# Polysketch attention with a gated feed-forward network: den in the idle accumulator bank, gating ahead of the division, one scratch write and GpSimd-issued reads, outer products of batch 0 in three pieces

## The chip, the cores and the metric

The kernel runs on one core of one Trainium2 chip. The metric is the device time of one execution in microseconds, the median of several runs. A profiled execution has its own time, and within it the span that the trace covers. Engines are named as the profile names them: PE multiplies matrices (PEld loads its weights), DVE is the vector engine, ACT the scalar engine, POOL is GpSimd, SP only issues transfers. SBUF is the memory on the core, PSUM holds what PE writes.

## The reference, cut to what matters

```python
q, k, v: (4, 4, 1088, 32)            # batch, heads, sequence, head_dim
S1, S2: (8, 32)
def phi(x):
    a = einsum('rd,bhsd->bhsr', S1, x)
    b = einsum('rd,bhsd->bhsr', S2, x)
    return einsum('bhsi,bhsj->bhsij', a, b).reshape(..., 64)
q_p, k_p = phi(q), phi(k)
kv  = einsum('bhsf,bhsd->bhfd', k_p, v)
z   = sum(k_p, axis=2)
num = einsum('bhsf,bhfd->bhsd', q_p, kv)
den = einsum('bhsf,bhf->bhs', q_p, z)[..., None] + 1e-06
x   = (num / den).transpose(0, 2, 1, 3).reshape(4352, 128)
out = (1 / (1 + exp(-(x @ w_gate))) * (x @ w_val)) @ w_out      # d_ff 1536
```

## The kernel before, in words

All arithmetic is in float32. The 4352 tokens of the feed-forward part are cut into eight chunks of 512 and one of 256. A **wave** (`w1`, L297) multiplies one chunk by one 128-wide tile of `w_gate` and of `w_val` (L309, two matmuls, four records in the trace). ACT takes the sigmoid of one half (L317), DVE multiplies it with the other (`glu`, L329, the gating, written `g`), and `w2` (L260) adds the product with the tile of `w_out` into an accumulator bank (L266). The accumulators have two PSUM banks, `acc0` and `acc1`, taken in turn by the chunks; when a chunk is done DVE turns it (L276) and SP stores it (L287). There are 102 waves. PE's queue runs `w2` two waves behind `w1`.

Between the waves stands the attention of the next batch, as groups handed to `slot` (L343): a group's instructions are issued first, then so many waves. The order of PE, DVE, ACT and POOL is the order in which the program is written; SP's queue has its own. For a batch `b`, `turn_k` and `turn_q` transpose the loaded k and q, `kps` (L386) projects k with S1 and S2, `outer` (L411) makes the 64 products of a token (`kp`), `kv` sums `kp` times `v`, `kvd` and `ndt` turn the result around into `nd` (numerator weights) and `zb` (denominator weights).

For q the products are made another way in most places: `qcomp` (L475) projects q, ACT copies the result to `cq`, `spread` (L504) writes `cq` to scratch memory in DRAM (`dq`) and reads it back twice, with rows repeated, as `qp` and `bq`; `qmult` (L539) multiplies the two on DVE. The query tokens of a batch are in two halves, `n` = 0 (8 blocks of 32 a parity) and `n` = 1 (9 blocks). `spread` does both halves of batches 1 to 3 in one go, and half 1 of batch 0 alone (`q01`). `bq` lies in the buffer that held the batch's k and q, and the next batch's k and q are loaded there after `qmult`. In batch 0, half 0, the projections are multiplied directly (`ab`).

`dn` (L636) then multiplies `qp` by `zb` (L644, the denominator) and by `nd` (L654, the numerator) into one two-bank PSUM tile of the pool `ps2`; for half 1 the denominator has to be cut into two pieces to fit beside the numerator. `divide` (L662) is six DVE steps: transposition of the denominator (`dT`, L665), + 1e-6 (L670), reciprocal (L671), transposition back (`rb`, L675), product with the numerator (`xT`, L684), and `xT` is what the waves multiply.

The weights come as 64-bit floating point words in pairs of 32-bit words and are narrowed on chip, tile by tile (`narrow`, L82, called as `narrow_w(j, step)`): POOL makes `cap` (L96), ACT `tail` (L100), DVE `head` in two instructions (L104, L108), ACT `square` (L116, into a PSUM tile that takes the bank `acc1`) and POOL adds `head` and `tail` (L117), DVE writes the float32 tile into `w_sb` (L120). Tile 0 is narrowed in two parts (`narrow_0`). Wave j of chunk 0 needs tile j, and the narrowing of the later tiles stands inside `w1` of chunk 0.

The program's start is batch 0: `outer` in four instructions (five and four of the nine key blocks), `kv0` (L544) after each, `kvd`, `ndt`, `dn(0, 0)`, `divide`, then the first wave. `warm` (L233) puts dummy matmuls on PE.

## Time and profile before

| what | value |
|---|---|
| median of 3 runs | 322.04 us (321.23 to 322.5) |
| profiled execution, its own time | 323.64 us |
| span of its trace | 321.8 us |
| PE busy | 303.6 us, 94% |
| DVE busy | 155.5 us, 48% |
| ACT busy | 80.4 us, 25% |
| POOL busy | 21.3 us, 7% |
| PE, waiting for DVE's gating (L266 behind L329) | 8.7 us in 8 waits |
| DVE, waiting for the reads of `bq` (L541) | 6.9 us in 2 waits |
| granted clock of PE, in tenths | 9 in every slice but one of 40, which has 7 |

The times of a row are the start in us from the start of the span and the length. PE's end is modelled: a matmul that follows another at once starts before the row of the one ahead has ended, so the length of a wave among others is best read from start to start. What an engine is said to wait for is the last to come; an idle stretch of an engine on which nothing waits costs nothing.

### The profile page before, as it was taken

To read this page: it belongs to the slowest core of one execution; us is meant where nothing else is said; L and a number is where in the kernel's file an instruction comes from. 1 tells how busy PE (TensorE), PEld (TensorE's weight loads), DVE (VectorE), ACT (ScalarE), POOL (GpSimd) and SP (SyncE) were. 2 spreads that over 40 slices of the span, in tenths; PEclk is the share of its full clock that TensorE was granted. 3 is DMA by queue.
4 is the path that set the end of the run, shared out by engine and by line. 5 is a ranking of instruction groups with operands and counts; after the bars stand their busy time and mean duration, and the time that the engine had idled before them with its cause. 6 is when DMAs were issued, how large, how long until landed. Compare 5 with 4: busy or idle time off the path is not lost.

```text
span 321.8 us, 3740 instructions
## 1 busy us (share of the span) xinstructions
PE 303.6 (94%) x1430; PEld 138.7 (43%) x1430; DVE 155.5 (48%) x268; ACT 80.4 (25%) x151; POOL 21.3 (7%) x36
## 2 busy tenths in 40 slices
PE   8868998999599999999999999999999999999994
PEld 2533443444234444443344444433444444444683
DVE  4778788763534645346446453464223222222331
ACT  2334552223011322221213222212122222222220
POOL 1235551000000000000000000000000000000000
PEclk9999999999979999999999999999999999999999
DMA  7990413177800257143002571010002000200021
GB/s 187 362 325 20 123 35 140 24 161 126 222 25 2 34 121 144 53 102 140 2 0 33 121 139 54 5 31 0 0 0 35 0 0 0 33 0 0 3 32 16
DMA packets 28656, 22.91 MB, mean 71 GB/s; under 512 B 19808, under 2 KB 23776, under 8 KB 28640
## 3 DMA queue, kind: packets, MB, share of 16 engines
q1 hardware_dynamic: 27712, 22.14, 27.7%
q10 hardware_dynamic: 928, 0.54, 0.8%
q8 instruction: 11, 0.18, 0.2%
q14 instruction: 5, 0.04, 0.0%
HBM read 19.46 MB, written 3.21 MB: 70 GB/s over the span
## 4 chain that ended last, share of the span: by engine, by line
PE 78%; DVE 10%; DMA 6%; issue 2%; SPq 1%; ACT 1%; POOL 1%; ACTq 0%; DVEq 0%
PE wave L309 46%; PE moeout L266 25%; DMA bq<-dq 5%; DVE rb L675 2%; DVE xT L684 2%; DVE g L329 2%; PE dn L654 1%; PE dn L644 1%; DVE dT L665 1%; DMA kq<-in_k_dram 1%; PE kvz L551 1%; PE kps L396 1%; SPq L526 1%; PE kvz L565 1%; DVE head L108 1%
## 5 line engine op out<-in xcount | busy, mean ns | idle before, releaser
L309 PE MATMUL wave<-xT,w_sb 128*128 128x512 f32 (+1 forms) x436 | 193.2, 569 | 2.5 <-DVE w_sb L120 1.5
L329 DVE TENSOR_TENSOR g<-wave,sg 128x512 f32<-128x512 f32 x102 | 70.3, 690 | 124.6 <-ACT sg L317 124.0
L309 PEld LDWEIGHTS wave<-xT,w_sb 128*128 128x128 f32 x436 | 82.9, 191 | 97.0 <-issue 89.2
L266 PE MATMUL moeout<-g,w_sb 128*128 128x512 f32 (+1 forms) x216 | 106.2, 579 | 8.7 <-DVE g L329 8.7
L317 ACT ACTIVATE sg<-wave 128x512 f32<-128x512 f32 x102 | 60.9, 597 | 213.2 <-PE wave L309 213.2
L266 PEld LDWEIGHTS moeout<-g,w_sb 128*128 128x128 f32 x216 | 39.0, 190 | 54.7 <-issue 35.3
L117 POOL TENSOR_TENSOR head<-head,tail 128x384 int32<-128x384 int32 (+3 forms) x14 | 13.4, 959 | 22.4 <-DVE head L108 12.0
L541 DVE TENSOR_TENSOR qp<-qp,bq 128x1152 f32<-128x1152 f32 (+1 forms) x7 | 9.1, 1294 | 6.9 <-DMA bq<-dq 6.9
L665 DVE STREAM_TRANSPOSE dT<-dn 128x256 f32<-128x256 f32 (+2 forms) x12 | 4.0, 357 | 14.0 <-PE dn L654 14.0
L415 DVE TENSOR_TENSOR kp<-kab 128x1152 f32<-128x1152 f32 (+2 forms) x10 | 10.7, 1096 | 0.0
L120 DVE SCALAR_TENSOR_TENSOR w_sb<-square,head 128x384 f32<-128x384 f32 x11 | 6.1, 555 | 4.4 <-POOL head L117 4.4
L108 DVE SCALAR_TENSOR_TENSOR head<-cap,head 128x384 int32<-128x384 int32 (+3 forms) x14 | 7.9, 565 | 0.5
L239 PE MATMUL warm<-ones 128*128 128x512 f32 (+1 forms) x10 | 7.2, 858 | 1.0 <-DVE hm L245 1.0
L276 DVE STREAM_TRANSPOSE o_sb<-moeout 128x512 f32<-128x512 f32 (+1 forms) x9 | 6.1, 680 | 2.6 <-PE moeout L266 2.5
L96 POOL TENSOR_SCALAR cap<-w_in 128x384 f32<-128x384 f32 (+2 forms) x13 | 7.0, 549 | 4.1 <-DMA w_in<-in_moe_w_val_dram 4.1
L100 ACT ACTIVATE tail<-w_in 128x384 int32<-128x384 uint32 (+2 forms) x13 | 6.5, 518 | 0.0
L654 PE MATMUL dn<-qp,nd 64*32 64x256 f32 (+1 forms) x128 | 6.1, 401 | 0.4 <-issue 0.4
L675 DVE STREAM_TRANSPOSE rb<-rc 128x576 f32<-128x576 f32 (+2 forms) x9 | 6.1, 680 | 0.3
L684 DVE TENSOR_TENSOR xT<-dn,rb 128x576 f32<-128x576 f32 (+2 forms) x9 | 6.0, 661 | 0.3
L373 DVE STREAM_TRANSPOSE kT<-kq 128x1088 f32<-128x1088 f32 (+2 forms) x5 | 5.4, 1070 | 1.3 <-DMA kq<-in_k_dram 1.3
L384 DVE STREAM_TRANSPOSE qT<-kq 128x512 f32<-128x512 f32 (+1 forms) x8 | 5.7, 714 | 0.0
L644 PE MATMUL dn<-qp,zb 128*32 128x256 f32 (+2 forms) x96 | 5.6, 338 | 0.1
(59 smaller groups left out, 81.7 us busy)
## 6 DMA issues: line engine op xcount, KB each, us to landing
v<-in_v_dram SPq DMA_DIRECT2D x16, 144.0 KB, 5.6
bq<-dq SPq DMA_DIRECT2D x8, 288.0 KB
qp<-dq SPq DMA_DIRECT2D x3, 576.0 KB, 10.6
kq<-in_k_dram SPq DMA_DIRECT2D x3, 544.0 KB
kq<-in_q_dram SPq DMA_DIRECT2D x3, 544.0 KB, 4.9
w_in<-in_moe_w_gate_dram SPq DMA_DIRECT2D x6, 256.0 KB
w_in<-in_moe_w_val_dram SPq DMA_DIRECT2D x6, 256.0 KB, 6.6
w_in<-in_moe_w_out_dram SPq DMA_DIRECT2D x6, 256.0 KB, 5.3
```

The costliest lines, as they stand in the source:

```text
L108: nc.vector.scalar_tensor_tensor(out=head, in0=cap, scalar=-0x40000000, in1=head, op0=ALU.bitwise_and, op1=ALU.bitwise_or)
L117: nc.gpsimd.tensor_tensor(out=head, in0=head, in1=tail, op=ALU.add)
L266: nc.tensor.matmul(out=moe["acc"][:, :tw], lhsT=w_sb[:, 2, j, :], rhs=g[:, jj, :tw], start=(j == 0), stop=(j == NJ - 1),)
L309: nc.tensor.matmul(out=wv[:, which, jj * tw + o : jj * tw + o + tp], lhsT=w_sb[:, which, j0 + jj, :], rhs=xT[:, t0 + o : t0 + o + tp], sta ...
L317: nc.scalar.activation(out=sg, in_=wv[:, 0], func=ACTF.Sigmoid)
L329: nc.vector.tensor_tensor(out=g, in0=wv[:, 1], in1=sg, op=MUL)
L415: nc.vector.tensor_tensor(out=KP[b][:, pi, j0:j1].rearrange("p j m (i l) -> p (j m) i l", i=R), in0=bass.AP(tensor=a0.tensor, offset=a0.of ...
L541: nc.vector.tensor_tensor(out=q0, in0=q0, in1=half(BQ[b], n), op=MUL)
L644: nc.tensor.matmul(out=t[32 * h : 32 * h + 32, i, w : w + 32 * (u1 - u0)], lhsT=zb[b % 2][:, h, :], rhs=half(QP[b], n)[:, 2 * (h % 2) + h ...
L654: nc.tensor.matmul(out=t[32 * h : 32 * h + 32, c, :w], lhsT=ND[b][rows, 32 * h : 32 * h + 32], rhs=half(QP[b], n)[rows, 2 * (h % 2) + h // ...
L675: nc.vector.transpose(out=rb[:, u0:u1].rearrange("p t c s -> p (t c s)"), in_=bass.AP(tensor=r0.tensor, offset=r0.offset, ap=[list(r0.ap[0 ...
L684: nc.vector.tensor_tensor(out=xT[:, o : o + 64 * (u1 - u0)].rearrange("p (t c s) -> p c t s", c=2, s=32), in0=t[:, :, 32 * u0 : 32 * u1].r ...
```

## The change

It has five parts.

1. The denominator goes into a PSUM tile of its own (`dps`), in the accumulator bank that the running chunk does not use: `acc0` or `acc1`, by the new entry `moe["sum"]`, the chunk whose `w2` began last. For half 1 it is four matmuls of 288 columns in place of eight of 224 and 64, and one transposition on DVE in place of two. The last weight tile's `square` goes to SBUF, so that `acc1` is free of it. The numerator keeps the tile of `ps2`.
2. `part` puts the gating of the wave before ahead of `dn` and `divide`, at seven of the eight divisions (all but the first of batch 0).
3. `spread` writes all of `cq` to scratch with one transfer and reads it back with eight transfers of 64 partitions (288 KB each) for both halves, four for one half. For batches 1 to 3 SP issues the write and POOL the reads; for `q01` ACT writes, SP reads. Both halves are 288 columns wide in scratch and in the buffers (`W1`), so half 0 carries 32 columns a row that nothing uses.
4. Batch 0's outer products come in six instructions (key blocks 0 to 3, 4 to 6, 7 and 8; two of the four heads in each), with `kv0` over all four heads after each pair.
5. Two steps of the narrowing of weight tile 1 stand before the first division, where they stood behind it.

```diff
+    W1 = 32 * q_chk[1][1]
...
-                narrowing[j] = narrow(w_sb[:, :, j, :], w_in[n][:, :, jj], nc.gpsimd, True)
+                narrowing[j] = narrow(w_sb[:, :, j, :], w_in[n][:, :, jj], nc.gpsimd, j < NJ - 1)
...
         if j0 == 0:
+            moe["sum"] = ci
             moe["acc"] = pso.tile([P, TCH], F32, tag=f"acc{ci % 2}", name="moeout")
...
-        w0, w1 = 32 * q_chk[0][1], 32 * q_chk[1][1]
-        if 0 in ns:
-            nc.scalar.copy(out=cq[:, :, :w0], in_=t[:, :, :w0])
-            nc.scalar.copy(out=cq[64:, :, w0:w1], in_=t[64:, :, w0:w1])
-        else:
-            nc.scalar.copy(out=cq[64:, :, :w1], in_=t[64:, :, :w1])
+        p0 = 64 * ns[0]
+        nc.scalar.copy(out=cq[p0:], in_=t[p0:, :, :W1])
...
+    def spread(b, ns, cq, put, get):
+        p0 = 64 * ns[0]
+        d = dram.tile([P, 2, W1], F32, tag="dq", name="dq")
+        put.dma_start(out=d[p0:], in_=cq[p0:])
         for n in ns:
             for c in range(2):
+                for i, t in enumerate((QP[b], BQ[b])):
+                    d0 = d[64 * n + 32 * c + 16 * i, 0]
+                    rows = [[4 * W1, R], [0, R]] if i == 0 else [[0, R], [4 * W1, R]]
+                    get.dma_start(
+                        out=t[64 * c : 64 * c + 64, n * H * W1 : (n + 1) * H * W1],
+                        in_=bass.AP(
+                            tensor=d0.tensor, offset=d0.offset, ap=rows + [[1, H * W1]]
+                        ),
                     )
...
-        t = ps2.tile([P, 2, 512], F32, tag="two", name="dn")
-        u = min(tn, (512 - w) // 32)
-        pieces = [(0, 0, u), (1, u, tn)] if u < tn else [(0, 0, tn)]
-        for i, u0, u1 in pieces:
-            for h in range(H):
-                nc.tensor.matmul(
-                    out=t[32 * h : 32 * h + 32, i, w : w + 32 * (u1 - u0)],
...
+        dps = pso.tile([P, TCH], F32, tag=f"acc{(moe['sum'] + 1) % 2}", name="dps")
+        for h in range(H):
+            nc.tensor.matmul(
+                out=dps[32 * h : 32 * h + 32, :w],
+                lhsT=zb[b % 2][:, h, :],
+                rhs=half(QP[b], n)[:, 2 * (h % 2) + h // 2, :],
+                start=True,
+                stop=True,
+            )
+        t = ps2.tile([P, 2, 512], F32, tag="two", name="nps")
...
-            for i, u0, u1 in pieces:
-                nc.vector.transpose(
-                    out=dT[:, u0:u1].rearrange("p t c -> p (t c)"),
-                    in_=t[:, i, w : w + 32 * (u1 - u0)],
-                )
+            nc.vector.transpose(out=dT[:, :tn].rearrange("p t c -> p (t c)"), in_=dps[:, :w])
...
-    outer(0, 0, 0, 5)
-    outer(0, 1, 0, 5)
-    kv0([1, 2, 3, 4, 0], range(H))
-    for pi in range(2):
-        outer(0, pi, 5, NJK)
-        kv0([5, 6, 7, 8], [2 * pi, 2 * pi + 1])
+    for j0, j1 in ((0, 4), (4, 7), (7, NJK)):
+        for pi in range(2):
+            outer(0, pi, j0, j1)
+        kv0([1, 2, 3, 0] if j0 == 0 else range(j0, j1), range(H))
...
+    narrow_w(1, 0)
     ndt(0)
     narrow_0(0, 2)
+    narrow_w(1, 1)
     warm(256)
     divide = dn(0, 0)
     warm(512)
-    narrow_w(1, 0)
...
-    narrow_w(1, 1)
...
-        spread(b, (0, 1), cq[b])
+        spread(b, (0, 1), cq[b], nc.sync, nc.gpsimd)
...
-        spread(0, (1,), qcomp(0, (1,), (ps2, "two")), nc.scalar, True)
+        spread(0, (1,), qcomp(0, (1,), (ps2, "two")), nc.scalar, nc.sync)
+
+    def part(b, n):
+        glu()
+        dn(b, n)()
...
-    slot(lambda: dn(0, 1)(), 2)
+    slot(lambda: part(0, 1), 2)
...
-        slot(lambda: dn(b, 0)(), wn)
+        slot(lambda: part(b, 0), wn)
         slot(None, 1)
-        slot(lambda: dn(b, 1)(), 4)
+        slot(lambda: part(b, 1), 4)
```

DVE's queue at the start of the program, before, from the turned key projections (`kab`) to the first division's denominator:

```order
L406 STREAM_TRANSPOSE kab<-kps 128x288 x2
L415 TENSOR_TENSOR kp<-kab 128x640 x2
L415 TENSOR_TENSOR kp<-kab 128x512 x2
L463 TENSOR_TENSOR qp<-bps,asb 128x2x256 x2
L104 TENSOR_SCALAR head<-cap 128x256
L108 SCALAR_TENSOR_TENSOR head<-cap,head 128x256
L631 COPY zb_144<-ndps 64x4 x2
L120 SCALAR_TENSOR_TENSOR w_sb<-cap,head 128x2x128
L665 STREAM_TRANSPOSE dT<-dn 128x256
```

And the same stretch of DVE's queue after the change:

```order
L409 STREAM_TRANSPOSE kab<-kps 128x288 x2
L418 TENSOR_TENSOR kp<-kab 128x512 x2
L418 TENSOR_TENSOR kp<-kab 128x384 x2
L418 TENSOR_TENSOR kp<-kab 128x256 x2
L465 TENSOR_TENSOR qp<-bps,asb 128x2x256 x2
L105 TENSOR_SCALAR head<-cap 128x256
L109 SCALAR_TENSOR_TENSOR head<-cap,head 128x256
L608 COPY zb_144<-ndps 64x4 x2
L105 TENSOR_SCALAR head<-cap 128x384
L109 SCALAR_TENSOR_TENSOR head<-cap,head 128x384
L121 SCALAR_TENSOR_TENSOR w_sb<-cap,head 128x2x128
L639 STREAM_TRANSPOSE dT<-dps 128x256
```

The two `head` instructions of weight tile 1 (384 columns), which stood behind the division, have moved up between `zb` and the first tile's `w_sb`, and the four outer products have become six.

DVE's queue at the second division of batch 0 (half 1), before, from the product of the two read-backs on (`w_sb` in the third row is that of weight tile 10; that of tile 11 comes right behind the last row):

```order
L541 TENSOR_TENSOR qp<-qp,bq 128x1152
L329 TENSOR_TENSOR g<-wave,sg 128x512
L120 SCALAR_TENSOR_TENSOR w_sb<-square,head 128x3x128
L104 TENSOR_SCALAR head<-cap 128x384
L108 SCALAR_TENSOR_TENSOR head<-cap,head 128x384
L665 STREAM_TRANSPOSE dT<-dn 128x224
L665 STREAM_TRANSPOSE dT<-dn 128x64
L670 TENSOR_SCALAR rc<-dT 128x18
L671 RECIPROCAL rc<-rc 128x18
L675 STREAM_TRANSPOSE rb<-rc 128x576
L684 TENSOR_TENSOR xT<-dn,rb 128x2x9x32
L329 TENSOR_TENSOR g<-wave,sg 128x512
```

The same stretch after the change, one row longer at its end (`w_sb` of tile 11):

```order
L518 TENSOR_TENSOR qp<-qp,bq 128x1152
L332 TENSOR_TENSOR g<-wave,sg 128x512
L121 SCALAR_TENSOR_TENSOR w_sb<-square,head 128x3x128
L105 TENSOR_SCALAR head<-cap 128x384
L109 SCALAR_TENSOR_TENSOR head<-cap,head 128x384
L332 TENSOR_TENSOR g<-wave,sg 128x512
L639 STREAM_TRANSPOSE dT<-dps 128x288
L641 TENSOR_SCALAR rc<-dT 128x18
L642 RECIPROCAL rc<-rc 128x18
L646 STREAM_TRANSPOSE rb<-rc 128x576
L655 TENSOR_TENSOR xT<-nps,rb 128x2x9x32
L121 SCALAR_TENSOR_TENSOR w_sb<-cap,head 128x3x128
```

The second gating, which stood behind `xT`, stands ahead of `dT`; `w_sb` of tile 11 follows `xT` directly. PE's first denominator matmul here now also waits for DVE (its bank `acc1` held `square` of tile 10, which the `w_sb` in the third row reads).

SP's queue for the spread of batch 1, before, from the scratch writes to the loads of the next batch's v:

```order
L513 DMA dq<-cq 32x1x256 x4
L513 DMA dq<-cq 16x576 x4
L526 DMA qp<-dq 128x1x1024
L526 DMA bq<-dq 64x1x1024 x2
L526 DMA qp<-dq 128x1x1152
L526 DMA bq<-dq 64x1x1152 x2
L287 DMA out_dram<-o_sb 32x16x32 x4
L197 DMA v<-in_v_dram 32x4x288 x4
```

SP's queue around the same place after the change, from the loads of that batch's k and q to those of the next:

```order
L185 DMA kq<-in_k_dram 128x1088
L185 DMA kq<-in_q_dram 128x1088
L503 DMA dq<-cq 128x576
L290 DMA out_dram<-o_sb 32x16x32 x4
L198 DMA v<-in_v_dram 32x4x288 x4
L185 DMA kq<-in_k_dram 128x1088
```

Of fourteen transfers one write is left on SP. The eight reads, `qp` and `bq` in turn, stand on POOL, whose queue holds nothing but the reads of batches 1 to 3 after its last narrowing step.

## Rows read from the trace of the kernel before

**Rows 1.** Waits of PE: who waited for whom: us in total, times, longest.

```profile
PE moeout L266 <- DVE g L329: 8.7, 8, 3.9
```

**Rows 2.** Timeline, first division of batch 2: start, us, instruction [idle before <-releaser].

```profile
148.50 1.88 PE L309 MATMUL wave<-xT,w_sb 128*128 128x512 f32 x4
...
150.04 0.68 DVE L329 TENSOR_TENSOR g<-wave,sg 128x512 f32<-128x512 f32 x1
...
150.78 1.12 PE L266 MATMUL moeout<-g,w_sb 128*128 128x512 f32 x2 [0.41 <-DVE g L329]
...
151.74 1.88 PE L309 MATMUL wave<-xT,w_sb 128*128 128x512 f32 x4
```

**Rows 3.** Chain that ended last, in order of time: start, us, what.

```profile
141.29 0.86 PE moeout L266 x2
142.15 1.72 PE wave L309 x4
```

**Rows 4.** Timeline, first division of batch 1.

```profile
81.56 1.88 PE L309 MATMUL wave<-xT,w_sb 128*128 128x512 f32 x4
...
83.04 1.36 DVE L541 TENSOR_TENSOR qp<-qp,bq 128x1152 f32<-128x1152 f32 x1 [4.97 <-DMA bq<-dq]
...
86.64 1.28 DVE L329 TENSOR_TENSOR g<-wave,sg 128x512 f32<-128x512 f32 x2
...
87.38 1.12 PE L266 MATMUL moeout<-g,w_sb 128*128 128x512 f32 x2 [3.94 <-DVE g L329]
...
88.34 3.23 PE L309 MATMUL wave<-xT,w_sb 128*128 128x512 f32 x4
```

**Rows 5.** Stretches: length, busy (count) of PE, PEld, DVE, ACT, POOL, PE clock, DMA share, GB/s.

```profile
88.50:91.58 3.08, 3.08 (x9) 0.79 (x11) 0.00 (x0) 0.00 (x0) 0.00 (x0) 0.54 0.16 64
```

**Rows 6.** Timeline of SP's queue: transfers issued for the spread of batch 1.

```profile
60.05 4.55 SPq L513 DMA_DIRECT2D dq<-cq  x8
64.70 0.54 SPq L526 DMA_DIRECT2D qp<-dq  x1
```

**Rows 7.** Chain that ended last, batch 1: the last read, from issue to landing.

```profile
67.92 15.00 DMA bq<-dq
```

**Rows 8.** Stretches while reads run: batch 1, then batch 2 (columns as in Rows 5).

```profile
66.00:68.00 2.00, 2.00 (x6) 0.80 (x6) 1.25 (x3) 0.60 (x1) 0.00 (x0) 1.00 1.02 279
126.00:128.00 2.00, 2.00 (x6) 0.83 (x5) 0.86 (x2) 0.60 (x1) 0.00 (x0) 1.00 0.51 147
```

**Rows 9.** Chain that ended last: key sums of batch 0, then of batch 2.

```profile
10.36 3.19 PE kvz L551 x140
134.20 1.28 PE kvz L565 x72
```

**Rows 10.** Timeline of the start, from the first division to the third wave.

```profile
17.33 0.45 DVE L665 STREAM_TRANSPOSE dT<-dn 128x256 f32<-128x256 f32 x1 [1.14 <-PE dn L654]
...
19.36 1.96 PE L309 MATMUL wave<-xT,w_sb 128*128 128x256 f32 x8 [1.02 <-DVE xT L684]
...
21.05 1.12 DVE L108 SCALAR_TENSOR_TENSOR head<-cap,head 128x128 int32<-128x128 int32 x1
...
22.79 1.95 PE L309 MATMUL wave<-xT,w_sb 128*128 128x512 f32 x4 [1.46 <-DVE w_sb L120]
...
25.66 1.13 PE L266 MATMUL moeout<-g,w_sb 128*128 128x512 f32 x2 [0.91 <-DVE g L329]
...
26.82 1.98 PE L309 MATMUL wave<-xT,w_sb 128*128 128x512 f32 x4
```

**Rows 11.** Timeline, second division of batch 0.

```profile
46.16 1.96 POOL L117 TENSOR_TENSOR head<-head,tail 128x384 int32<-128x384 int32 x1 [1.62 <-ACT square L116]
...
47.58 0.70 PE L644 MATMUL dn<-qp,zb 128*32 128x224 f32 x16
...
48.15 0.56 DVE L120 SCALAR_TENSOR_TENSOR w_sb<-square,head 128x384 f32<-128x384 f32 x1 [0.29 <-POOL head L117]
...
52.79 1.13 PE L266 MATMUL moeout<-g,w_sb 128*128 128x512 f32 x2 [1.10 <-DVE g L329]
```

More of the change, by code (lines that the diff above doesn't have):

```diff
@@ L483, in qcomp @@
                     nc.tensor.matmul(
-                        out=t[32 * g : 32 * g + 32, pi, : 32 * tn],
+                        out=t[32 * g : 32 * g + 32, pi, :W1],
                         lhsT=skq[rows, :],
-                        rhs=qT_of[b][rows, t0 : t0 + tn, c, :],
+                        rhs=qT_of[b][rows, t0 : t0 + W1 // 32, c, :],
                         start=True,
@@ L506, in spread @@
         for n in ns:
-            w = 32 * q_chk[n][1]
-            d = ds[n] = dram.tile([2, 2, R, H, w], F32, tag=f"dq{n}", name="dq")
             for c in range(2):
-                p0 = 64 * n + 32 * c
-                for i in range(2):
-                    if not ci:
-                        eng.dma_start(
-                            out=d[i, c].rearrange("r (m p) w -> (r m) p w", m=2),
-                            in_=cq[p0 + 16 * i : p0 + 16 * i + 16, :, :w],
-                        )
-                if ci:
-                    eng.dma_start(
-                        out=d[c].rearrange("i r (m p) w -> (i r m) p w", m=2),
-                        in_=cq[p0 : p0 + 32, :, :w],
-                    )
@@ L522, in spread @@
-        for n in ns:
-            hw = H * 32 * q_chk[n][1]
-            def read(t, d0, p0, pn, rows):
-                nc.sync.dma_start(
-                    out=half(t, n)[p0 : p0 + pn].rearrange("p h w -> p (h w)"),
-                    in_=bass.AP(tensor=d0.tensor, offset=d0.offset, ap=rows + [[1, hw]]),
-                )
-            d = ds[n]
-            if not ci:
-                read(QP[b], d, 0, P, [[hw, 2 * R], [0, R]])
-            for c in range(2):
-                if ci:
-                    read(QP[b], d[c, 0], 64 * c, 64, [[hw, R], [0, R]])
-                read(BQ[b], d[c, 1] if ci else d[1, c], 64 * c, 64, [[0, R], [hw, R]])
+                for i, t in enumerate((QP[b], BQ[b])):
[6 more added lines that the diff above has]
+                        ),
+                    )
```

29 lines of the change are left out of this document (10 added, 19 removed).

## The prediction, made before the changed kernel was run

> **What bounds the kernel now.** I read the busy times first: PE is busy for nearly all of the span, so a microsecond is worth something only where PE stands still or runs slowly, and the question for each part is which of PE's idle stretches it removes. The list of PE's waits gives them: 8.7 us in eight waits of `w2` for DVE's gating [rows 1]. The timelines around these waits show why. At a division DVE's queue holds the six division steps ahead of the gating that PE needs next [rows 2]; at the first division of batch 1 it holds, ahead of those, a product that waits for a read of `bq` [rows 4]. After that long idle stretch PE's granted clock is 0.54, the lower of its two levels (1.2 of 2.4 GHz) for most of the next wave [rows 5]. What is left is the start: there the chain runs through DVE, ACT and POOL, and PE's third wave begins only at 26.82 [rows 10]. From then on PE is the bound wherever it does not wait.
>
> The measure of a lost stretch is start to start. Undisturbed, a wave takes 1.72 us of PE and a `w2` 0.86 [rows 3]. Around the wait of 0.41 us in batch 2 the wave's start and the next `w2`'s lie 150.78 - 148.50 = 2.28 apart and the next wave follows after 0.96 [rows 2]: (2.28 - 1.72) + (0.96 - 0.86) = 0.66 lost, that is the wait plus 0.25 us.
>
> **The change, part by part.**
>
> *Gating ahead of the division.* Of the eight waits, 3.94 belongs to batch 1's read [rows 4], 1.10 to batch 0's second division [rows 11], 0.91 to the start [rows 10]. That leaves 8.7 - 5.95 = 2.75 us in five waits, one a division. With the gating ahead, `w2` finds it done: its sigmoid comes from a wave that ended before `dn` began. What is late next is the gating of the following wave, now behind the division, but PE needs it one wave and one `w2` (2.58 us) later than the one that was moved. Saved: 2.75 + 5 x 0.25 = **4.0 us**. Cover gone elsewhere: DVE's division ends 0.68 us later (one gating [rows 2]); `xT` is wanted only waves later, except in batch 0, below.
>
> *`dps` in the idle bank.* In half 1 the denominator keeps its 288 columns, in half as many matmuls; PE's time there goes by columns, so nothing. One DVE transposition fewer, hidden. The bank must be free. In batches 1 to 3 its last user is a chunk that ended waves before: nothing. In batch 0's second division it is `acc1`, with `square` of weight tile 10, read by a `w_sb` that ran from 48.15 to 48.71, while `dn` began at 47.58 [rows 11]. So PE now waits 1.13 + 0.25 there, the next `w2` and wave behind it, where it lost 1.10 + 0.25 before. Net **0**; at best 1.35 gained (if that `w_sb` comes sooner), at worst 0.5 lost, since `w_sb` of tile 11 now stands behind the whole division and the wave that needs it comes next.
>
> *One write, reads from POOL.* SP issued eight writes in 4.55 us, 0.57 each, then the reads from 64.70 on [rows 6]; the last landed at 67.92 + 15.00 = 82.92 [rows 7]. Now one write goes out at about 60.05, and reads can follow between 60.6 and 64.7; I take 62.5 for its landing. No row shows POOL issuing a transfer. Lower bound: SP's 0.54 us [rows 6]. Upper bound: POOL's slow instruction in these rows, 1.96 us [rows 11]. Eight reads are issued by 62.5 + 8 x 0.54 = 66.8 or by 78.2; POOL has no other work by then. The data, 8 x 288 KB = 2.30 MB, take 8.3 us at 279 GB/s or 15.7 at 147 [rows 8], so they land between 70.8 and 78.2 by rate, or up to 3 us (estimate) after the last issue, 81.2 at the latest. At the average of before (2.18 MB from 64.70 to 82.92, 119 GB/s) it would be 81.9. When must they be there? PE's `w2` is due at 81.56 + 1.72 = 83.28 [rows 3, 4]; ahead of it DVE needs the product, 1.36, and one gating, 0.68: 81.2. So nearly the whole span of bounds ends before the wait begins. I take 77, near the 147 GB/s row, because it was measured with half the engines busy while such reads ran. Then PE loses nothing: saved are (87.38 - 81.56 - 1.72) + 0.10 = 4.2 us, and the slow clock, 3.23 - 1.88 = 1.35 [rows 2, 4]: **5.6 us**. In batches 2 and 3 no wait for reads is in PE's list and each has more waves between spread and use. The 32 unused columns of half 0 cost 6% of bytes, counted above. SP's stores and loads of v, which stood behind the reads, now go out beside them and share the engines; that is why I do not take the fast end.
>
> The share of 0.51 with 147 GB/s [rows 8] says that half the transfer engines work when the reads of `bq` are alone. The Trainium skill (DMA: Bandwidth & Descriptors, section "Why a DMA increments its semaphore by 16 and not by 1") has a rule for this: a transfer uses the largest number of engines up to 16 that divides the slowest dimension of both sides, here the eight-fold repetition, and such a transfer from GpSimd takes eight consecutive engines from a cursor that moves on. By that rule alternate reads would share all sixteen and land near 71, and the first rival below would fall to 1 in 10; the sum stays as it is.
>
> *Batch 0's products in three pieces, and the division's start.* Three steps. (a) The key sums took 3.19 us for 140 records, 22.8 ns each, the second part with two heads at a time; with four heads throughout, as in batch 2, it is 1.28 / 72 = 17.8 ns [rows 9]: 2.5 us. With a first pair of products that is shorter I take 0.8 saved. (b) `dT` waited until 17.33 for the numerator's matmuls, with DVE idle for 1.14 us [rows 10]; in its own bank the denominator no longer waits for them. The two narrowing steps that move up fill that idle time. From `dT` to the first wave it is 2.03 us [rows 10]; `dT` can start between 15.5 and 16.2, and the numerator ends at 17.3 - 0.8, so the first wave starts 1.1 to 1.9 earlier. I take 1.7 (0.8 of it from (a)). (c) From the first wave to the third it is 26.82 - 19.36 = 7.46 us; PE's own work in it is two waves and a `w2`, 4.3 [rows 3, 10]. In the excess of 3.16 lie the wait of 1.46 for weight tile 1, the wait of 0.91 for the gating, and a 128-column instruction on DVE of 1.12 us [rows 10], all behind narrowing steps that now run before the division. DVE, ACT and POOL still narrow tile 2 there, so not all goes: I take 2.3, bounds 0.3 and 3.1. Sum **4.0 us**, bounds 1.4 and 5.0.
>
> **Sum.** 4.0 + 0 + 5.6 + 4.0 = 13.6 us. The profiled execution, 321.8 us of span and 1.84 around it, would go from 323.64 to 310.0; the median of the runs lies 1.60 below that execution, so 322.04 - 13.6 = **308.4 us**.
>
> **Rivals.**
>
> *The reads land no sooner (82.92).* For it: the engines set the pace, and SP's stores now run beside the reads. Against it: reads start earlier and the rows reach 279 GB/s. Then the moved gating ends at 82.92 + 0.10 + 1.36 + 0.68 = 85.06 in place of 87.32; PE loses 1.8 + 0.25, then about 1.0 as the next gating waits behind the division, and the clock still falls: 4.4 of the 5.6 us stay. 312.8 us.
>
> *The start is held by narrowing as before.* For it: every tile passes DVE, ACT and POOL in turn, and the 1.12 us instruction shows that DVE and POOL hold each other up [rows 10]. Against it: DVE and POOL idle before the first division. Only 1.4 is gained: 311.0 us.
>
> *Slower: POOL issues slowly.* Each read takes T on POOL, and the place is again the first division of batch 1. Landing is 62.5 + 8T + 3, so PE's loss is 62.5 + 3 + 2.04 - 83.28 + 8T, plus 0.25, 1.0 and 1.4 as above: 8T - 13.1. Against the 5.6 of before and with 8.0 saved elsewhere the kernel is slower when 8T is over 26.7, T over 3.3 us; at T = 4 it is 5.3 us slower, 327.3 us. For it: a POOL instruction of 384 columns took 1.96 us while DVE multiplied `qp` by `bq` [rows 4, 11]. Against it: even 1.96 would do. The Trainium skill (SBUF: State Buffer, "Who interferes with whom", and the box on the trap that DVE blocks DMA) speaks against this part: GpSimd writes the descriptors itself and is locked out while DVE holds a shared port, 3100 ns where 620 would do. By its figure T would be 3.1 and the time an estimated 320.1 us; no row here shows a POOL-issued transfer.
>
> **How the numbers follow.** Forecast 60%; reads no sooner 18%; start held 13%; POOL slow 9%, of which 2 near its turning point. The range reaches down by the rest of the start's bound (1.0) and part of the bank's (0.8), to 306.6, and up past the first rival to 313.4; outside lie the slow POOL and little else. A difference under 0.5% (1.6 us) can't be told from none here: faster 0.91, same 0.02, slower 0.07.
>
> **What the profile after would show.** The waits of PE for the gating all but gone; the clock at 1.00 after batch 1's first division; the last `bq` of batch 1 landed before 81 less the start's gain; a new wait of PE for DVE of about 1.1 us at the second division of batch 0; the third wave at about 22.8. I am wrong if POOL's reads are issued over 2 us apart, if DVE waits for `bq` again, or if the waits at the start move to the next narrowing step.

## The result, and the profile after

The changed kernel took **309.24 us**, the median of four executions (308.58 to 310.0), beside 321.63 us (320.91 to 322.5) for the kernel before in the same comparison: a ratio of 0.9614, with a 95% interval of 0.9578 to 0.965. The prediction was 308.4 us, in a range of 306.6 to 313.4. The profiled execution took 310.0 us over a span of 308.2, 13.6 less than before, which is the sum forecast. By the medians the gain is 12.4 us here and 13.6 in a later comparison (322.95 against 309.36). How the 13.6 divide is another matter: below, two terms turn out to have been each other's doubles.

The page after: busy time of each engine; PE's granted clock in 40 slices; the product of `qp` and `bq` with its idle time; the reads, now issued by POOL, with the KB of each and the median time to landing.

```profile
PE 299.1 (97%) x1398; PEld 136.9 (44%) x1398; DVE 155.3 (50%) x266; ACT 80.0 (26%) x148; POOL 34.6 (11%) x60
PEclk9999999999999999999999999999999999999999
L518 DVE TENSOR_TENSOR qp<-qp,bq 128x1152 f32<-128x1152 f32 (+1 forms) x7 | 9.1, 1293 | 1.5 <-DMA bq<-dq 1.5
qp<-dq POOLq DMA_DIRECT2D x12, 288.0 KB, 8.8
bq<-dq POOLq DMA_DIRECT2D x12, 288.0 KB, 9.1
```

PE's share went from 94% to 97% and no slice has the lower clock. POOL's count is now 60, 24 more, which are the reads that it issues. The list of PE's waits (in all us, times, longest) holds, where `w2` had 8.7 us in eight [rows 1]:

```profile
PE dps L618 <- DVE w_sb L121: 1.1, 1, 1.1
PE nps L629 <- issue: 1.0, 1, 1.0
PE moeout L269 <- DVE g L332: 0.2, 1, 0.2
```

The timeline of batch 1's first division shows the place of the largest loss before [rows 4]:

```profile
76.25 0.64 PE L618 MATMUL dps<-qp,zb 128*32 128x256 f32 x8
76.35 1.36 DVE L518 TENSOR_TENSOR qp<-qp,bq 128x1152 f32<-128x1152 f32 x1 [1.47 <-DMA bq<-dq]
77.62 0.68 DVE L332 TENSOR_TENSOR g<-wave,sg 128x512 f32<-128x512 f32 x1
78.37 1.88 PE L312 MATMUL wave<-xT,w_sb 128*128 128x512 f32 x4
...
80.09 1.02 PE L269 MATMUL moeout<-g,w_sb 128*128 128x512 f32 x2
```

DVE still waits for a read, 1.47 us, but the gating stands right behind the product and ends at 78.30, 1.8 us before `w2` needs it at 80.09. PE waits for nothing.

To compare runs I cut each trace at PE instructions that all of them have. T0 is the start of the first transposition of the key projections (`kab` on DVE; what comes before it hangs on the first loads), W3 the start of the third wave, "division b.n" the start of the denominator's matmuls of batch b, half n. In us, each from one profiled execution:

| kernel | T0 | T0 to W3 | W3 to div. 1.0 | div. 1.0 to 1.1 | div. 1.1 to 3.1 | div. 3.1 to end |
|---|---|---|---|---|---|---|
| before | 8.02 | 18.80 | 52.62 | 12.06 | 128.96 | 101.31 |
| after | 8.69 | 15.13 | 52.43 | 6.50 | 125.50 | 99.95 |
| after, once more | 9.63 | 15.53 | 52.43 | 6.51 | 125.50 | 99.95 |
| gating alone | 7.60 | 18.83 | 52.25 | 7.36 | 125.50 | 100.38 |
| bank alone | 8.23 | 17.75 | 52.65 | 9.18 | 126.19 | 100.60 |
| reads alone | 8.15 | 18.96 | 52.61 | 7.18 | 128.68 | 101.77 |
| gating undone | 7.47 | 14.91 | 52.68 | 8.49 | 126.18 | 100.18 |
| bank undone | 7.38 | 16.05 | 52.21 | 6.52 | 125.50 | 99.95 |
| spread undone | 8.03 | 15.16 | 52.43 | 6.88 | 125.50 | 101.35 |
| reads on SP | 8.17 | 15.18 | 52.44 | 8.09 | 125.50 | 100.38 |
| products undone | 8.23 | 15.65 | 52.41 | 7.07 | 125.50 | 99.94 |
| narrowing undone | 8.29 | 17.07 | 52.45 | 6.51 | 125.49 | 99.95 |
| tile 11 ahead | 7.60 | 15.17 | 51.82 | 6.50 | 125.50 | 99.93 |
| tile 11 inside | 7.73 | 14.91 | 51.25 | 6.51 | 125.49 | 99.94 |

The columns from the third wave on repeat to 0.02 us between the two executions of the changed kernel. The start does not: where its code is the same, T0 to W3 lies between 14.91 and 15.53, so that differences under 0.6 us are not told apart in that column. T0 lies between 7.38 and 9.63, by the landing of the first loads, and the whole trace moves with it. Of the difference between before and after, -0.67 is T0, 3.67 the start, 0.19 the stretch to division 1.0, 5.56 the stretch from division 1.0 to 1.1, 3.46 that from there to division 3.1, 1.36 the end: 13.6. Of the 1.36, 0.44 lies behind DVE's last instruction, where only the last stores are left.

### The profile page after: what moved, and what is told of

The parts are those of the page before. It is cut to its first block, busy times and chain, and to the rows that moved or that the text cites. A ratio compares the mean times of both kernels' runs of the same rounds, so it can differ in the third digit from the quotient of the medians.

```text
span 308.2 us, 3676 instructions
## 1 busy us (share of the span) xinstructions
PE 299.1 (97%) x1398; PEld 136.9 (44%) x1398; DVE 155.3 (50%) x266; ACT 80.0 (26%) x148; POOL 34.6 (11%) x60
## 4 chain that ended last, share of the span: by engine, by line
PE 90%; DVE 4%; DMA 2%; POOL 1%; ACT 1%; SPq 0%; issue 0%; POOLq 0%; ACTq 0%; DVEq 0%
PE wave L312 55%; PE moeout L269 29%; DMA kq<-in_q_dram 2%; PE nps L629 1%; PE dps L618 1%; PE kvz L542 1%; DVE kp L418 1%; POOL head L118 1%; PE cqps L485 1%; PE kps L399 1%; DVE w_sb L121 1%; DVE head L109 0%; DVE qp L465 0%; DVE xT L655 0%; DVE rb L646 0%
## 5 line engine op out<-in xcount | busy, mean ns | idle before, releaser
L509 POOL DMA_DIRECT2D qp<-dq x12 | 7.0, 584 | 110.2 <-DMA dq<-cq 110.2
L418 DVE TENSOR_TENSOR kp<-kab 128x1152 f32<-128x1152 f32 (+3 forms) x12 | 11.1, 956 | 0.0
L109 DVE SCALAR_TENSOR_TENSOR head<-cap,head 128x384 int32<-128x384 int32 (+3 forms) x14 | 7.1, 506 | 0.5
L629 PE MATMUL nps<-qp,nd 64*32 64x256 f32 (+1 forms) x128 | 6.1, 401 | 1.0 <-issue 1.0
L509 POOL DMA_DIRECT2D bq<-dq x12 | 6.9, 576 | 0.3
L618 PE MATMUL dps<-qp,zb 128*32 128x256 f32 (+1 forms) x64 | 5.3, 404 | 1.2 <-DVE w_sb L121 1.1
L655 DVE TENSOR_TENSOR xT<-nps,rb 128x576 f32<-128x576 f32 (+2 forms) x9 | 6.0, 662 | 0.9
```

The costliest lines, as they stand in the source:

```text
L418: nc.vector.tensor_tensor(out=KP[b][:, pi, j0:j1].rearrange("p j m (i l) -> p (j m) i l", i=R), in0=bass.AP(tensor=a0.tensor, offset=a0.of ...
L509: get.dma_start(out=t[64 * c : 64 * c + 64, n * H * W1 : (n + 1) * H * W1], in_=bass.AP(tensor=d0.tensor, offset=d0.offset, ap=rows + [[1, ...
L618: nc.tensor.matmul(out=dps[32 * h : 32 * h + 32, :w], lhsT=zb[b % 2][:, h, :], rhs=half(QP[b], n)[:, 2 * (h % 2) + h // 2, :], start=True, ...
L629: nc.tensor.matmul(out=t[32 * h : 32 * h + 32, c, :w], lhsT=ND[b][rows, 32 * h : 32 * h + 32], rhs=half(QP[b], n)[rows, 2 * (h % 2) + h // ...
```

## The experiments

**Gating undone.** The changed kernel without the moved call, at all seven divisions:

```
     def part(b, n):
-        glu()
         dn(b, n)()
```

> The changed kernel with one part undone: at the five divisions behind the start the gating stands behind the division again, as in the kernel before. Theory: PE waits for DVE's gating again at each division, as it did before: 0.41 to 0.67 us of wait plus 0.25 us each, 4.0 us in all by the prediction's working; at the first division of batch 1 DVE's queue now holds a product that waits for a read until 76.35, so the gating behind it comes later still, up to 1 us more there. Expected 4.0 to 5.3 us slower than the changed kernel, about 314 us, with waits of w2 for the gating in five places. Rival (the order is worth nothing once the reads are early and PE has the next wave to do): within 0.8 us of the changed kernel, 309 to 310 us, no such waits.

Measured: 313.72 us, but its four executions spread from 311.71 to 315.84, with a mean granted clock of 1.00 in the shorter two and 0.995 in the others; which stretch ran slower no trace shows. In the profiled one (311.71) one wait of `w2` is left, not five:

```profile
80.78 1.13 PE L269 MATMUL moeout<-g,w_sb 128*128 128x512 f32 x2 [1.72 <-DVE g L332]
```

By stages it lost 1.99 us from division 1.0 to 1.1 and 0.68 from there to division 3.1, where the waits of 0.41 to 0.67 us ought to have come back. Part of the 1.99 is a later read: DVE's product began 1.32 us behind the denominator's matmuls here (76.38 and 75.06), 0.10 us behind them in the changed kernel. With the read as early as there some 0.8 us would be left (an estimate, 1.99 - 1.22). Both theories missed: the order of the gating is worth something, but most of the five waits was taken away by another part as well. The timing alone would have looked like a confirmation.

**Gating alone.** The kernel before with `glu()` put ahead of `dn(b, n)()` at the same seven divisions, nothing else.

> The kernel before with one part of the change alone: the gating ahead of the five divisions behind the start; writes, reads, banks and start as before. Theory: the five waits of 0.41 to 0.67 us go, 4.0 us; at the first division of batch 1, where the gating now waits for the reads by the product ahead of it and no longer behind six division steps, another 1.0 to 1.8 us; at batch 0's second division another 1.1 us, since no bank is waited for there. Expected 4.0 to 6.9 us faster than the kernel before, 315 to 318 us. Rival (the gating waits are only passed on: the next gating, now behind the division, is late for the next w2): 0 to 1.5 us faster, 320 to 322 us, with new waits of w2 one wave further on.

Measured: 313.51 us (312.9 to 314.93), ratio 0.9752 (0.9688 to 0.9816): some 9.7 us, where 4.0 to 6.9 were expected. The reads go out as before, and land late; yet the timeline of batch 1's first division is:

```profile
80.81 1.88 PE L309 MATMUL wave<-xT,w_sb 128*128 128x512 f32 x4
81.25 1.36 DVE L541 TENSOR_TENSOR qp<-qp,bq 128x1152 f32<-128x1152 f32 x1 [3.94 <-DMA bq<-dq]
82.53 0.68 DVE L329 TENSOR_TENSOR g<-wave,sg 128x512 f32<-128x512 f32 x1
83.27 1.12 PE L266 MATMUL moeout<-g,w_sb 128*128 128x512 f32 x2 [0.58 <-DVE g L329]
84.23 1.88 PE L309 MATMUL wave<-xT,w_sb 128*128 128x512 f32 x4
...
85.45 0.68 DVE L329 TENSOR_TENSOR g<-wave,sg 128x512 f32<-128x512 f32 x1
86.04 0.70 PE L644 MATMUL dn<-qp,zb 128*32 128x224 f32 x16
...
87.31 1.12 PE L266 MATMUL moeout<-g,w_sb 128*128 128x512 f32 x2
```

DVE waits 3.94 us for the read, PE 0.58. The wave at 84.23 has its normal 1.88, where it took 3.23 before [rows 4]. The gating that now stands behind the division ends at 86.13, and its `w2` is due only at 87.31, because PE has the second division's matmuls first. Of the 5.56 us at batch 1 this order alone gives 4.70.

**Bank alone.** The kernel before with the denominator in the idle bank:

```
-        t = ps2.tile([P, 2, 512], F32, tag="two", name="dn")
+        dps = pso.tile([P, TCH], F32, tag=f"acc{(moe['sum'] + 1) % 2}", name="dps")
...
+        t = ps2.tile([P, 2, 512], F32, tag="two", name="nps")
```

> The kernel before with one part of the change alone: the denominator in the idle accumulator bank; the gating stays behind the division, reads and start as before. Theory formed after the first runs: DVE's transposition of the denominator starts while PE still works on the numerator, some 0.7 us sooner, and that alone ends most of the gating waits: 0.5 to 0.9 us saved at each of the five divisions behind the start, about 1 us at the start, 0.6 us more at batch 1's first division: 3.5 to 5.5 us faster than the kernel before, 316.5 to 318.5 us, waits of w2 for the gating in batches 2 and 3 under 0.2 us each. Rival (the prediction's step: the bank is worth nothing by itself, the waits of 0.41 to 0.67 us stay): 0 to 1.3 us faster, all of it at the start.

Measured: 317.49 us (316.23 to 320.31), ratio 0.9854 (0.9795 to 0.9913): the theory's range, and its profile has from 30 us on only two waits of PE:

```profile
PE moeout L267 <- DVE g L330: 2.4, 1, 2.4
PE dps L642 <- DVE w_sb L120: 1.1, 1, 1.1
```

The first is batch 1's read, the second batch 0's bank. No gating is waited for in batches 2 and 3. Batch 2's first division shows why; the first row is from the trace before, the others from this run:

```profile
147.71 0.45 DVE L665 STREAM_TRANSPOSE dT<-dn 128x256 f32<-128x256 f32 x1 [1.16 <-PE dn L654]
```

```profile
142.41 0.45 DVE L663 STREAM_TRANSPOSE dT<-dps 128x256 f32<-128x256 f32 x1 [0.53 <-PE dps L642]
...
143.83 1.88 PE L310 MATMUL wave<-xT,w_sb 128*128 128x512 f32 x4
...
144.82 0.68 DVE L330 TENSOR_TENSOR g<-wave,sg 128x512 f32<-128x512 f32 x1
145.56 1.12 PE L267 MATMUL moeout<-g,w_sb 128*128 128x512 f32 x2
```

In a tile of its own the denominator can be transposed while PE still works on the numerator: DVE is idle for 0.53 us in place of 1.16, the six steps end 0.6 us sooner, and the gating behind them ends at 145.50, where `w2` is due at 143.83 + 1.72 = 145.55. The bank and the moved gating buy the same 0.4 to 0.7 us.

**Reads alone.** The kernel before with one scratch write and reads from POOL, in the new layout of `qp` and `bq`:

```
-        spread(b, (0, 1), cq[b])
+        spread(b, (0, 1), cq[b], nc.sync, nc.gpsimd)
```

> The kernel before with one part of the change alone: one scratch write and reads issued by POOL; the gating stays behind the division, the denominator beside the numerator, the start as before. Theory formed after the first runs: the reads land some 6 us sooner, but with the gating behind the six division steps w2 still waits at batch 1's first division, for 2 to 2.5 us; 2.5 to 3.8 us saved there, nothing elsewhere: 318 to 319.5 us. Rival (the prediction's step, 5.6 us from the reads alone): about 316.5 us, no wait of w2 over 1 us at batch 1's first division.

Measured: 319.11 us (318.51 to 324.70), ratio 0.9889 (0.9854 to 0.9923). The time is the theory's, its reason is not: the waits of `w2` stay (from 30 us on seven, 4.3 us, none over 1.1), and batch 1's read is early, so that its division is like any other.

```profile
78.27 1.35 DVE L518 TENSOR_TENSOR qp<-qp,bq 128x1152 f32<-128x1152 f32 x1
84.13 1.13 PE L269 MATMUL moeout<-g,w_sb 128*128 128x512 f32 x2 [0.41 <-DVE g L332]
```

At batch 1 it saves 4.88 us: at this place the rival is right, and taken by itself the reads' term was nearly as large as predicted. The time is above the rival's all the same; 0.45 us of it lie behind DVE's last instruction (4.32 against 3.86 us).

**Spread undone.** The changed kernel with the eight writes, the old layout and SP's reads.

> The changed kernel with one part undone: eight small writes of the scratch and reads issued by SP, in the layout of the kernel before; the gating, the denominator's bank and the start stay as changed. Theory: the reads of batch 1 land at 82.9 less the 3.2 us by which everything ahead of them is earlier, 79.7; the moved gating ends 2.1 us later, 81.9, against a due time of w2 of 83.3 - 3.2 = 80.1: PE waits about 1.8 us, loses 0.25 us beside it, waits about 1.0 us for the following gating and then runs at the lower clock for most of a wave, 1.0 to 1.4 us. Expected 3 to 4.5 us slower than the changed kernel, 312.3 to 313.8 us. Rival (the reads were never late once the gating stands ahead of the division; the time at batch 1 came from the gating): within 0.8 us of the changed kernel, 309 to 310 us, granted clock 1.00 behind the division.

Measured: 311.01 us (310.73 to 311.16), ratio 0.9665 (0.9596 to 0.9734): between the two. At batch 1 it loses 0.38 us, and the wave behind the division runs at full speed. There the rival is right: with the other parts in place the new spread is worth 0.4 us in this profile; between "gating alone" and after, which has the bank and the new start besides, it is 0.86. Both are within the scatter of the landings (last section). The other 1.40 us, which neither theory named, lie behind DVE's last instruction; the last section comes back to them.

**Reads on SP.** The changed kernel with one word changed:

```
-        spread(b, (0, 1), cq[b], nc.sync, nc.gpsimd)
+        spread(b, (0, 1), cq[b], nc.sync, nc.sync)
```

> The changed kernel with one edit: the reads of batches 1 to 3 are issued by SP in place of POOL; the one write and the layout stay. Theory (the single write is what counts: it lets the reads start some 4 us sooner, whoever issues them): the reads of batch 1 start at about 59.3 to 59.5 and land by 77.5 at the latest, PE loses at most 0.5 us and the time is within 0.7 us of the changed kernel. Rival (what counts is that POOL's transfers use all 16 transfer engines where SP's use half): DMA's share while the reads run alone falls from about 1.0 to about 0.5, at 147 GB/s the 2.36 MB take 16 us and with SP's stores in the same queue more, landing after 78; DVE's product then waits 2 to 4 us longer, PE waits 1 to 3 us, and the time is 311 to 313 us.

Measured: 310.37 us (309.89 to 311.57), ratio 0.9654 (0.9591 to 0.9716), 1.59 us lost at batch 1. By its waits the rival holds; the time lies below its 311 to 313 us and above the theory's. The rows of one stretch (its length; busy time and count of PE, PEld, DVE, ACT, POOL; clock; DMA share; GB/s) of the changed kernel and of this run, while the reads are under way:

```profile
66.00:68.00 2.00, 2.00 (x6) 0.95 (x5) 1.55 (x4) 0.60 (x1) 0.00 (x0) 1.00 1.06 173
```

```profile
66.00:68.00 2.00, 2.00 (x6) 0.95 (x5) 1.14 (x3) 0.60 (x1) 0.00 (x0) 1.00 0.63 166
...
68.00:70.00 2.00, 2.00 (x78) 1.12 (x76) 0.56 (x1) 0.60 (x1) 0.00 (x0) 1.00 0.50 147
```

From SP about half of the transfer engines work, from POOL all. DVE's product waits until 79.09, 20.5 us after the first read is issued, and PE waits:

```profile
81.11 1.12 PE L269 MATMUL moeout<-g,w_sb 128*128 128x512 f32 x2 [1.31 <-DVE g L332]
```

So one write with reads from SP came out worse than the spread of before (1.59 against 0.38 us): the reads start 2.5 us earlier, counted from the denominator's matmuls, and that is more than lost while about half of the engines work. Both figures are from one profile each, and the landing of the same POOL reads scatters (last section).

**Bank undone.** The changed kernel with the denominator beside the numerator again.

> The changed kernel with one part undone: the denominator stands again beside the numerator in one tile of two banks, and waits for that tile in place of the idle accumulator bank. Theory: at the start the denominator's transposition waits again for the numerator's matmuls, which puts the first wave 0.7 to 1.0 us later; at batch 0's second division the 1.1 us wait of PE for a weight sum goes, worth up to 1.35 us. The two nearly cancel: -0.6 to +0.3 us beside the changed kernel, with the third wave of the start 0.5 to 1.0 us later and the lead regained at 46. Rival (the start is set by the narrowing of the weights, not by the denominator): the third wave comes at the same time within 0.2 us and the kernel is 0.9 to 1.4 us faster than the changed one.

Measured: 310.35 us (309.38 to 310.59), ratio 0.9612 (0.9583 to 0.9641). The start is 0.92 us longer (0.5 to 1.1 by the scatter of that column), and the wave waits 1.02 us for `xT` as before [rows 10]. At batch 0's second division the bank's wait is gone, and the next tile's is there:

```profile
49.86 1.98 PE L312 MATMUL wave<-xT,w_sb 128*128 128x512 f32 x4 [0.70 <-DVE w_sb L121]
```

So the stretch to division 1.0 gains 0.22 and not the 1.1 of the wait: the start went as the theory had it, the cancelling did not. In the changed kernel the bank is worth 0.7 us by these stages and 1 us by the medians, all of it at the start.

**Products undone.** Batch 0's outer products in two pieces again.

> The changed kernel with one part undone: batch 0's products of keys and values in two pieces with key sums of two heads at a time, as before, in place of three pieces. Theory of the prediction: the key sums then take 0.8 us longer and every wave of the start comes 0.8 us later; the time is 0.5 to 0.9 us above the changed kernel. Rival (the first loads and the products on DVE set the start, not the sums on PE): within 0.3 us.

Measured: 309.39 us (309.22 to 310.61), ratio 0.9595 (0.9565 to 0.9625). The denominator's matmuls come 7.01 us behind T0, as before (7.00), against 6.18 in the changed kernel: that is the theory's 0.8 us. At the third wave 0.5 are left, 0.1 to 0.7 by the scatter of that column. The remaining 0.57 at batch 1 comes with a late read; nothing shows that this edit made it late:

```profile
78.58 1.36 DVE L518 TENSOR_TENSOR qp<-qp,bq 128x1152 f32<-128x1152 f32 x1 [3.65 <-DMA bq<-dq]
...
80.59 1.12 PE L269 MATMUL moeout<-g,w_sb 128*128 128x512 f32 x2 [0.30 <-DVE g L332]
```

By the times it can't be told from the changed kernel (309.24 and 309.36), as the rival had it.

**Narrowing undone.** `narrow_w(1, 0)` and `narrow_w(1, 1)` behind the first division again.

> The changed kernel with one edit undone: the two narrowing steps of weight tile 1 stand behind the first division of batch 0 again. Theory: the second wave waits for tile 1 again; the stretch from the first wave to the third, 7.46 us before and 5.18 in the changed kernel, grows by 1.5 to 2.3 us, and the time with it: 310.7 to 311.6 us. Rival (the division's own matmuls in the idle bank freed the start, and the narrowing only filled idle time): the stretch grows by less than 0.6 us, the time by less than 0.6 us.

Measured: 311.61 us (311.2 to 313.03), ratio 0.9664 (0.9629 to 0.9699). First wave to third is 7.22 us, against 5.18 after and 7.46 before, and both waits are back:

```profile
21.32 1.95 PE L312 MATMUL wave<-xT,w_sb 128*128 128x512 f32 x4 [1.30 <-DVE w_sb L121]
24.19 1.12 PE L269 MATMUL moeout<-g,w_sb 128*128 128x512 f32 x2 [0.92 <-DVE g L332]
```

The theory holds. This edit is the largest single piece of the start, 1.94 us (1.5 to 2.2 by the scatter of that column).

**A step further.** What is left in the changed kernel is the wait of 1.1 us for the bank. First, tile 10's squares in SBUF (`j < NJ - 2` for `j < NJ - 1`) and the weight sum of tile 11 ahead of the division:

```
     def part(b, n):
         glu()
+        if (b, n) == (0, 1):
+            narrow_w(11, 3)
         dn(b, n)()
```

> A step further than the change: the squares of weight tile 10 are kept in SBUF like those of the tiles ahead of it, so that the idle accumulator bank is free at batch 0's second division, and the weight sum of tile 11 is put ahead of that division. Theory: the 1.1 us wait of PE for the weight sum of tile 10 and 0.25 us beside it go, and no wait takes their place: 1.0 to 1.4 us faster than the changed kernel, about 308.0 us. Rival (the next wave waits for tile 11, whose narrowing DVE and POOL only finish behind the division): a wait of the wave of 0.8 to 1.1 us in the same place, the time within 0.4 us of the changed kernel.

Measured: 308.61 us (308.16 to 308.85), ratio 0.956 (0.9532 to 0.9588). Half of the gain expected: the stretch falls by 0.61 us. The wait for the bank is gone, but DVE idles 0.60 us for POOL ahead of that sum, and the gating behind the division is then late for `w2` by 0.30. So the sum was put inside the division, behind the reciprocal:

> The run with tile 11 ahead of batch 0's second division, one step further: the weight sum of tile 11 stands inside the division, behind the reciprocal, where DVE does not have to wait for POOL. Theory: DVE's idle 0.6 us ahead of that sum is filled by the division's first steps, the following gating comes 0.6 us sooner and the wait of 0.30 us, with the lateness around it 0.57 us, goes: 0.3 to 0.6 us below that run, 1.0 to 1.4 us below the changed kernel of the same call. Rival (the next wave then waits for tile 11): no better than that run, a wait of the wave for the weight sum.

Measured: **307.98 us** (307.53 to 308.27), ratio 0.9546 (0.9511 to 0.9581); the changed kernel in the same comparison

> The changed kernel once more, as the yardstick for the small differences of the other runs: 308.5 to 310 us, with the stages of its first profile (from the start of the denominator's matmuls of batch 1's first division to those of its second 6.5 us, and 53.7 us from there to batch 2's first) repeated within 0.1 us; only the first loads and the last stores may move the total, by about 1 us.

took 309.36 us (308.72 to 311.39), ratio 0.9596 (0.9552 to 0.9639), its stages from the third wave on repeated to 0.02 us, its start 0.40 us longer. The executions of the two don't overlap; 1.18 of the 1.4 us is the stretch to division 1.0, and the rest is no more than the scatter of the start. At batch 0's second division nothing waits any more:

```profile
43.40 0.69 PE L619 MATMUL dps<-qp,zb 128*32 128x288 f32 x8
...
46.81 0.49 DVE L121 SCALAR_TENSOR_TENSOR w_sb<-cap,head 128x384 f32<-128x384 f32 x1
...
49.92 1.02 PE L269 MATMUL moeout<-g,w_sb 128*128 128x512 f32 x2
```

This version is faster than both kernels.

## Why the prediction was right, and where it was right by luck of overlap

**Gating ahead, 4.0 us.** Right in size: in "gating alone" the stretches behind division 1.1 shrink by 3.46 + 0.93 = 4.4 us, and the next gating is not late, as the prediction argued.

**The bank, net 0.** Right for the sum and for batch 0: the new wait came where and as long as forecast (1.11 us against 1.13), and the stretch gained 0.19.

```profile
45.76 0.69 PE L618 MATMUL dps<-qp,zb 128*32 128x288 f32 x8 [1.11 <-DVE w_sb L121]
```

But the step "One DVE transposition fewer, hidden" failed as a reading. The prediction saw that the denominator no longer waits for the numerator, and used it at the start only; the same holds at every division. Alone, the bank saves 2.88 us at batch 1 and 2.77 from division 1.1 to 3.1. It counts for nothing behind the start only because the moved gating takes the same waits.

**One write, reads from POOL, 5.6 us.** The place gave 5.56 us, but not by the reads. Alone, the gating gives 4.70, the reads 4.88, the bank 2.88; all together 5.56. Undoing the gating costs 1.99 there (some 0.8 of it by the order itself, the rest by a later read), undoing the spread 0.38, undoing the bank 0.02. The prediction gave the moved gating nothing at this wait and the reads all of it. The failed step is the price in the first rival, "4.4 of the 5.6 us stay" if the reads land no sooner. Its first half was right: in "gating alone" PE lost 0.74 at the wait (0.58 and some lateness around it) with reads that landed 1 us sooner than that rival assumed. The "about 1.0" for the next gating is not there, since PE has the second division's 1.27 us first, and the clock stays at 2.4 GHz behind the 0.58 us: the next wave takes its 1.88. "Spread undone" and "gating alone" show 0.4 and 0.9 us lost at this place by late reads, where that rival had 4.4; the range's upper end hung on this and was too high.

**The reads' own course.** First issue was predicted at 62.5, that is 59.3 with the 3.2 us by which the trace is ahead there; it came at 59.29. POOL's time for each lay near the lower bound:

```profile
59.29 0.73 POOL L509 DMA_DIRECT2D qp<-dq  x1 [11.55 <-DMA dq<-cq]
...
60.57 0.56 POOL L509 DMA_DIRECT2D qp<-dq  x1
...
63.26 0.60 POOL L509 DMA_DIRECT2D bq<-dq  x1
```

Landing was mis-sized: 77 would be 73.8 in this trace, and DVE's wait ended at 76.35. (The later of its bounds by rate, 78.2, ought to be 78.6: 8 x 288 KB are 2.36 MB in the units of the rates, not 2.30.) It cost nothing, because the deadline (81.2, here 78.0) was later still. The prediction had named "if DVE waits for `bq` again" as a sign of being wrong. DVE did wait, 1.47 us, and PE lost nothing: the sign was too strict, since only what reaches PE counts.

The rival of a slow POOL is settled by these rows. DVE ran instructions with two inputs from SBUF beside them (at 60.20 a product for 1.35 us, at 62.77 a sum for 1.22), and no issue took over 0.73. The prediction had read the Trainium skill (SBUF: State Buffer, "Who interferes with whom", and the box on the trap that DVE blocks DMA) as speaking against this part. That reading was wrong: the box is on instructions in a two-port mode, which the section says such a `tensor_tensor` doesn't have, and by the section a probe didn't see it stall a transfer; these rows agree. (POOL's own additions do slow down beside such a product: 1.96 us for 384 columns [rows 11], 0.99 for the one ahead of it.) The Trainium skill's other rule (DMA: Bandwidth & Descriptors, section "Why a DMA increments its semaphore by 16 and not by 1"), that such reads from GpSimd take eight engines from a moving cursor, fits the DMA share of 1.06 from POOL against about 0.5 from SP, though no row tells which engines a read used. The landing near 71 that was worked out from it (67.8 in this trace) did not follow, since all engines together moved 173 GB/s where I had taken 279.

**The start, 4.0 us.** Counted from T0 it is 3.67. (a) The key sums: 0.82, predicted 0.8. (b) The first wave: 11.34 to 9.95 us behind T0, 1.39 against 1.7. (c) From first wave to third: 2.28 against 2.3, shown to be the narrowing by its own run. The timeline, to be read beside [rows 10]:

```profile
16.43 0.45 DVE L639 STREAM_TRANSPOSE dT<-dps 128x256 f32<-128x256 f32 x1
...
17.07 0.63 PE L629 MATMUL nps<-qp,nd 64*32 64x256 f32 x6 [0.99 <-issue]
17.63 1.13 PE L241 MATMUL warm<-ones 128*128 128x512 f32 x2
...
18.16 0.42 DVE L655 TENSOR_TENSOR xT<-nps,rb 128x256 f32<-128x256 f32 x1
...
18.64 3.78 PE L312 MATMUL wave<-xT,w_sb 128*128 128x256 f32 x12
...
23.82 1.98 PE L312 MATMUL wave<-xT,w_sb 128*128 128x512 f32 x4
```

`dT` no longer waits. Counted from T0 it starts 1.57 us sooner than before, and 16.43 less the 0.67 us of T0 is inside the 15.5 to 16.2 forecast; but from `dT` to the first wave it is 2.21 us against 2.03. The wave is now held from two sides, which the prediction didn't see: the first part of `xT` is ready at 18.58, and PE reaches the wave at 18.64 without idle time, behind a pause of 0.99 us in the numerator's matmuls and the dummy matmuls of `warm`. In "tile 11 inside" that part of `xT` was ready at 17.42 and PE came to the wave only at 17.85: there a faster DVE would have gained nothing. The third wave came at 23.82 and not 22.8 in part because this execution's T0 was 0.67 us late. That loss and the 0.44 us gained behind DVE's last instruction were not in the sum and nearly cancel.

## What to carry to other kernels

Two edits that pull the same late instruction forward are not added: price each with the other in place, and look for the wait that both remove. Before a late operand is given a price, follow the queue behind it to where PE really needs the result; here the order of the queue alone left 0.9 us of the 5.6 that a late read had cost. A tile shared by two results made the reader of the first wait for the second at every division, not only where the trace showed the longest wait.

## What the runs showed of the hardware

The same eight reads from POOL, at the same place, took between at most 15.5 us ("reads alone", without a wait) and 19.2 us ("products undone") from first issue to the product's start, over the same bytes. In the two-microsecond stretches from about the last issue on "reads alone" moved 199 to 248 GB/s (66 to 76 us), the changed kernel 168 to 178 (64 to 76) and "products undone" 145 to 151 (64 to 76), all three at a DMA share of 0.92 to 1.09: a high share does not tell the rate. Nothing in these traces says why. Against this scatter the margin of some 1.8 us is small, and single profiles don't price the reads. Over all profiles they do better: counted from the denominator's matmuls of division 1.0, DVE's product began between 1.45 us ahead and 2.29 behind with POOL's reads, beyond that margin in one of nine, and 2.0 to 3.6 us behind with the spread of before, beyond it in all four.

PE's clock fell to the lower level after 3.94 us of idle time in the kernel before [rows 4, 5]; after 2.41 us (bank alone) and 1.72 us (gating undone) the profiled executions stayed at 2.4 GHz. Other executions of these two kernels have a mean clock down to 0.987 and are up to 4.1 us longer than the shortest; whether that is the same place was not traced.

T0 varied by 2.2 us with the landing of the first loads; between the two profiles of the changed kernel, 1.35 us apart in span, 0.94 lie there and 0.40 in the start. From the end of DVE's last instruction to the end of the span, where every kernel issues the same four stores, it took 3.40 to 3.42 us in eight of the nine profiles with POOL's reads (4.32 in "reads alone") and 3.84 to 3.86 in four of the five with SP's (4.82 in "spread undone"). That the issuer of reads that landed long before should matter there was not expected. The records place the difference on POOL, between its last clear of semaphores and its last drain (they start at 320.9 and 321.4 us before, at 307.8 and 307.9 after); in "spread undone" one wait of SP ahead of it took 1.30 us. No run tells why.

At batch 0's first division the numerator's matmuls pause after ten of sixteen, for 0.42 to 0.58 us where the key sums are in two pieces and 0.85 to 1.31 where they are in three, with no releaser in the trace. In all fourteen profiles the pause ended 8.3 to 8.8 us behind T0, although the denominator's matmuls began anywhere from 6.1 to 7.0 us behind it: most of the 0.82 us that the key sums gained was waited away again on PE. The DMA view lists one transfer of the kind `instruction` shortly before; for the changed kernel between 14.5 and 15.5 us (count, MB, share of the 16 engines):

```profile
q8 instruction: 1, 0.02, 6.9%
```

Its 16 KB took 1.07 to 1.15 us, beside the loads of the weights, and in all fourteen the matmuls went on 1.26 to 1.57 us after its end. That PE waits there for its instructions fits, but is not shown; no run moved this transfer.
